# Attention with a gated expert layer: laying out the keys and queries of the first two pairs by products with the identity

## The chip, the cores and the metric

The kernel runs on one core of one Trainium2 chip. The metric is the device time of one execution in microseconds (us); three executions of the kernel before took 623.07, 626.6 and 625.8 us, with a median of 625.8.

## What is computed

Inputs are q, k and v of 4 batches, 8 heads, 576 positions and 64 dimensions, in float32. The reference, cut to what matters:

```
scores = q @ k.T / 8
x      = log1p(|i - j|) / log1p(max(i, 1))           # one number per pair of positions
bias   = relu(x * w1 + b1) @ w2                       # 32 hidden units, 8 heads
attn   = softmax(scores + bias);  y = attn @ v        # y: 2304 tokens x 512
e      = argmax(y @ w_gate)                           # one of 8 experts per token
out    = gate * sigmoid((y @ w_output_gate)[e]) * (relu(y @ w1[e]) @ w2[e])
```

## The kernel before

The program has three parts in order of time. The first, up to about 75 us, makes the bias of all heads, once for all batches. The second walks through 16 pairs of heads (4 batches x 4 pairs) and makes attention. The third runs the experts on groups of 288 tokens. Each engine issues its instructions in the order in which the code emits them, and so does SyncE (SP), which only issues transfers. A wait is set automatically wherever data or a buffer needs one.

**Bias rows.** A loop over 36 steps `r16` (line 957) makes 16 rows of positions in each step. `emit_hid` (713) makes four tiles of hidden units, two steps ahead; the digits of `ON_ACT` (71) say how many of the four ScalarE makes, VectorE makes the rest. The tile `hid` has three buffers. `emit_bias` (730) has TensorE multiply them by `w2` into one of two PSUM banks (tag `s`, shared with the scores), ScalarE evicts the result into one of four places (`evs`, line 731: step r uses the place of step r-4), and SyncE stores it from there into `bias`.

**Work laid between the bias rows.** `BEGIN` (66) names what is begun after which step: `l` and `L` load the second and third pair (`emit_load`, 758, two SyncE transfers of k and q into one tile `nat`, of which there is one buffer, line 159); `k0` to `k2` and `K0` to `K2` lay out the first and the second pair in three chunks; `p0` to `p2` and `P0` to `P2` move parts of them; `s0` to `s3` make the first scores, `z` copies a part of the queries on GpSimd, `v` loads the values. What a step begins is finished in the next step, after that step's `emit_hid` and ahead of its `emit_bias`. Behind the loop the string `FIRST` (52) orders the rest of the first pair; its `k0++`, `k1++`, `k2++` lay out the third pair, which must have been loaded by then.

**Keys and queries.** The score product wants three operands of 128 partitions: the keys rounded, twice, one copy in each half of 64 partitions; the keys' remainder, twice; and the queries, rounded above and their remainder below. `emit_kq` (798) transposes one chunk of `nat` (keys above, queries below), ScalarE writes the rounded values (`hi`), VectorE the remainder (`lo`). `emit_place` (812) then moves halves to where they belong with SyncE transfers of 288 KB, four for a pair: two in `p0`, one in `p1` that overwrites what `p0` reads, one in `p2`.

Of the kernel before, what the change touches and what calls it, by code (L numbers as in the profile page):

```python
# [9 lines left out]
F32 = mybir.dt.float32  # L10
F32R = mybir.dt.float32r
# [3 lines left out]
ACTF = mybir.ActivationFunctionType  # L15
ALU = mybir.AluOpType
# [4 lines left out]
B, H, S, D = 4, 8, 576, 64  # L21
# [42 lines left out]


BEGIN = {
    3: "k0", 4: "k1", 5: "k2 l", 7: "p0", 9: "p1", 13: "p2 K0", 14: "z", 16: "K1", 17: "s0", 20: "K2",
    21: "L", 22: "s2 s1", 29: "P0", 32: "s3 P1", 35: "v P2",
}

ON_ACT = "210210000111121212102110310010201111"
# [63 lines left out]
def attention_moe_kernel(  # L135
# [15 lines left out]
    nc = tc.nc  # L151
    V = nc.vector
# [19 lines left out]
    def cn(name):  # L172
        o, n = _WHERE[name]
        return kept[:, o:o + n]

    ident = cn("ident")
# [8 lines left out]
    def psum_t():  # L185
        return ps_t.tile([128, 512], F32, name="pt", tag="t")
# [485 lines left out]
    with ExitStack() as actx:  # L672
        pool = lambda name, bufs, **kw: actx.enter_context(tc.tile_pool(name=name, bufs=bufs, **kw))
        kq = pool("kq", 2)
# [81 lines left out]
        kl_t, v_t, vb_t, nat_t = {}, {}, {}, {}  # L756

        def emit_load(b, pr):
            t = nat_t[b, pr] = nat.tile([128, 9, 2, D], F32, name="nat", tag="nat")
            for i, x in enumerate((k, q)):  # L760
                nc.sync.dma_start(
                    out=t[:, :, i, :],
                    in_=x[b, 2 * pr:2 * pr + 2].rearrange("h s d -> (h s) d").rearrange("(n p) d -> p n d", p=128),
                )

        def emit_load_v(b, pr):
            vt = vp.tile([128, 9, D], F32, name="vt", tag="v")
            nc.sync.dma_start(
                out=vt, in_=v[b, 2 * pr:2 * pr + 2].rearrange("h s d -> (h s) d").rearrange("(n p) d -> p n d", p=128)
            )  # L770
            v_t[b, pr] = vt
# [26 lines left out]
        def emit_kq(b, pr, c):  # L798

            hi, lo = (t[(b * NPAIR + pr) % 2][:, c * 384:c * 384 + 384] for t in (kh2, qs2))  # L800
            pt = psum_t()
            for i in range(3):
                nc.tensor.transpose(  # L803
                    pt[:, i * 128:i * 128 + 128], nat_t[b, pr][:, c * 3 + i].rearrange("p t d -> p (t d)"), ident
                )
            nc.scalar.activation(out=hi, in_=pt[:, 0:384], func=ACTF.Copy, scale=cn("ksc"))
            yield
            V.scalar_tensor_tensor(
                out=lo, in0=pt[:, 0:384], scalar=cn("ksc"), in1=hi.bitcast(F32), op0=ALU.mult, op1=ALU.subtract
            )  # L810

        def emit_place(b, pr, i):

            hi, lo = (t[(b * NPAIR + pr) % 2] for t in (kh2, qs2))
            if i == 0:
                kl_t[b, pr] = kq.tile([128, 2 * S], F32R, name="kl", tag="kt")
            kl, up, down = kl_t[b, pr], slice(0, 64), slice(64, 128)
            for to, src in (((kl[up], lo[up]), (kl[down], lo[up])), ((lo[up], hi[down]),), ((hi[down], hi[up]),))[i]:
                nc.sync.dma_start(out=to.bitcast(F32), in_=src.bitcast(F32))

        def emit_q4(b, pr):
            nc.gpsimd.tensor_copy(
                out=q4.rearrange("p (a c) -> p a c", c=64)[:, 0::3, :],
                in_=qs2[(b * NPAIR + pr) % 2].rearrange("p (h c) -> p h c", h=2)[:, :, 512:S].bitcast(F32),
            )
# [14 lines left out]
        def emit_s(b, pr, qb, hl):  # L840
            h = 2 * pr + hl
            if b not in sums_t:
                sums_t[b] = st_p.tile([128, 4, H], F32, name="sums", tag="sums", bufs=2)
                sums4_t[b] = st_p.tile([128, NPAIR], F32, name="sums4", tag="sums4", bufs=2)
            e_t[b, pr, qb] = e_all[qb]
            ps = ps_s.tile([128, 2, 512], F32, name="ps", tag="s")
            kt, qs = (x[(b * NPAIR + pr) % 2] for x in (kh2, qs2))
            low = kl_t[b, pr]
            o = hl * S + qb * 128
            k0 = hl * S  # L850
            for c in range(2):
                for n, keys in enumerate((kt, low)):
                    nc.tensor.matmul(  # L853
                        ps[:, c, 0:288], lhsT=qs[:, o:o + 128], rhs=keys[:, k0 + c * 288:k0 + c * 288 + 288],
                        start=n == 0, stop=n == 1,
                    )
            yield
            softmax_rows(e_t[b, pr, qb][:, hl, :], ps, bias[qb][:, h, :], sums_t[b][:, qb, h:h + 1])
# [66 lines left out]
        pairs = [(b, pr) for b in range(B) for pr in range(NPAIR)]  # L925
        begun = " ".join(BEGIN.values()).split()

        def begin(op):
            if op[0] == "k":
                return emit_kq(*pairs[0], int(op[1]))  # L930
            elif op[0] == "p":
                emit_place(*pairs[0], int(op[1]))
            elif op[0] == "s":
                return emit_s(*pairs[0], int(op[1]) // 2, int(op[1]) % 2)
            elif op[0] == "K":
                return emit_kq(*pairs[1], int(op[1]))
            elif op[0] == "P":
                emit_place(*pairs[1], int(op[1]))
            elif op in "lL":
                emit_load(*pairs[1 + (op == "L")])  # L940
            elif op == "v":
                emit_load_v(*pairs[0])
            elif op == "z":
                emit_q4(*pairs[0])
            return iter(())
# [11 lines left out]
        for r16 in range(36):  # L957
            if r16 < 34:
                hids.append(emit_hid(r16 + 2))

            for g in halfway:
                finish(g)
            halfway.clear()
            emit_bias(r16, hids.pop(0))
            for op in BEGIN.get(r16, "").split():
                g = begin(op)
                next(g, None)
                halfway.append(g)
# [3 lines left out]
        for hl in range(2):  # L972
            for i, w in enumerate((wg, wog)):
                nc.sync.dma_start(
                    out=wgb[hl * 64:hl * 64 + 64, :, hl * 16 + i * 8:hl * 16 + i * 8 + 8],
                    in_=w.rearrange("(a t d) e -> t d a e", t=2, d=64)[hl],
# [24 lines left out]
        for n in range(len(pairs) + 1):  # L1001
            todo = {i: 1 for i in range(8)}
            for op in orders.get(n, ORDER).split():
                name = op.rstrip("+-")
# [19 lines left out]
                b, pr = pairs[m]  # L1024
                i = int((name + "0")[1])
# [12 lines left out]
                elif name[0] == "t":  # L1038
                    emit_t(
                        b, pr, i, int(name[2]), copies("a" if name[0:3] in to_act and b == B - 1 and m < len(pairs) - 1 else name[3])  # L1040
                    )
                elif name[0] == "a":
                    emit_av(b, pr, i, copies(name[2]))
                    if i == 2 and m == len(pairs) - 2:
                        emit_zb(*pairs[-1])
                    if pr == NPAIR - 1:
                        work.append(emit_logits(b, i))
                        if i == 2:
                            work.append(emit_route(b))
                            if b >= B - 2:  # L1050
                                work.append(route_group(b - (B - 2)))
                elif name[0] in "kp":
                    if name[0] == "p":
                        emit_place(b, pr, i)
                    else:
                        finish(emit_kq(b, pr, i))
                else:
                    {"l": emit_load, "v": emit_load_v, "c": emit_z, "b": emit_load_vb, "g": emit_zb, "z": emit_q4}[name](b, pr)
# [201 lines left out]
```

## Time and profile before

| | before |
|---|---|
| median of three executions | 625.8 us |
| profiled execution | 619.93 us, of which the span 617.8 |
| TensorE products (PE) | 576.8 us busy, 93% of the span |
| weight loads (PEld) | 489.2 us, 79% |
| VectorE (DVE) | 413.1 us, 67% |
| ScalarE (ACT) | 375.2 us, 61% |
| GpSimd (POOL) | 94.7 us, 15% |
| chain that ended last | PE 76%, no visible wait 6%, DVE 6%, DMA 5%, ACT 4% |

The profile describes one execution; its span runs from the first instruction to the last. Busy shares are means over parts of the program with different limits. Products overlap in the array, so TensorE's busy time also covers the latency of single products. A float32 product of the bias rows stands in the trace as two records.

### The profile page before, as it was taken

To read this page: it belongs to the slowest core of one execution; us is meant where nothing else is said; L and a number is where in the kernel's file an instruction comes from. 1 tells how busy PE (TensorE), PEld (TensorE's weight loads), DVE (VectorE), ACT (ScalarE), POOL (GpSimd) and SP (SyncE) were. 2 spreads that over 40 slices of the span, in tenths; PEclk is the share of its full clock that TensorE was granted. 3 is DMA by queue.
4 is the path that set the end of the run, shared out by engine and by line. 5 is a ranking of instruction groups with operands and counts; after the bars stand their busy time and mean duration, and the time that the engine had idled before them with its cause. 6 is when DMAs were issued, how large, how long until landed. Compare 5 with 4: busy or idle time off the path is not lost.

```text
span 617.8 us, 13534 instructions
## 1 busy us (share of the span) xinstructions
PE 576.8 (93%) x5070; PEld 489.2 (79%) x5070; DVE 413.1 (67%) x974; ACT 375.2 (61%) x774; POOL 94.7 (15%) x172
## 2 busy tenths in 40 slices
PE   4868799999999999999999899999999999999992
PEld 2323478888888778887777668999999999999992
DVE  6967676666777677776678756767777665555521
ACT  5788677777776677777677554535445454545410
POOL 1000000000010000100002382040404132120202
PEclk9988899999999999999999999999999999999997
DMA  6998976564566754586435675566666574756521
GB/s 142 228 204 191 228 161 140 125 135 102 125 140 167 157 123 109 116 211 134 108 102 130 199 256 179 173 213 197 199 185 203 174 221 145 248 158 181 168 69 48
DMA packets 99093, 100.26 MB, mean 162 GB/s; under 512 B 71319, under 2 KB 71575, under 8 KB 99016
## 3 DMA queue, kind: packets, MB, share of 16 engines
q1 hardware_dynamic: 93028, 84.93, 54.6%
q0 software_dynamic: 3232, 9.64, 4.9%
q10 hardware_dynamic: 2756, 4.72, 2.2%
q8 instruction: 42, 0.69, 0.5%
q14 instruction: 35, 0.29, 0.2%
HBM read 60.34 MB, written 9.50 MB: 113 GB/s over the span
## 4 chain that ended last, share of the span: by engine, by line
PE 76%; issue 6%; DVE 6%; DMA 5%; ACT 4%; POOL 1%; POOLq 0%; SPq 0%; DVEq 0%; ACTq 0%
PE p L1114 15%; PE p L1137 15%; PE pa L922 13%; PE ps L853 9%; PE pt L890 9%; PE pb L735 2%; PE ps L869 2%; PE pt L803 2%; DVE e L833 2%; DMA bias<-evh 2%; DVE hid L724 2%; PE pt L655 1%; PE pt L1156 1%; PE pt L902 1%; PE pt L515 1%
## 5 line engine op out<-in xcount | busy, mean ns | idle before, releaser
L838 ACT ACTIVATE e<-e,nm 128x576 f32<-128x576 f32 x144 | 111.3, 773 | 48.9 <-DVE nm L833 47.5
L833 DVE CUSTOM_DVE_ANT_0 e<-ps,bias 128x576 f32<-128x576 f32 x144 | 105.5, 751 | 32.4 <-PE ps L853 28.5
L1114 PE MATMUL p<-x,w 128*128 128x288 f32 x768 | 105.7, 296 | 0.0
L1114 PEld LDWEIGHTS p<-x,w 128*128 128x128 f32 x768 | 102.8, 188 | 0.5 <-issue 0.4
L890 PE MATMUL pt<-kept,e 128*128 128x128 f32 x576 | 82.8, 277 | 2.8 <-ACT et L894 1.2
L853 PE MATMUL ps<-qt,qs 128*128 128x288 f32 x256 | 79.3, 329 | 4.4 <-DVE nm L833 3.0
L890 PEld LDWEIGHTS pt<-kept,e 128*128 128x128 f32 x576 | 65.3, 141 | 18.0 <-issue 8.1
L1137 PE MATMUL p<-hh,w2h 128*128 128x288 f32 x256 | 77.3, 302 | 0.0
L1137 PE MATMUL p<-hl,w2h 128*128 128x288 f32 x256 | 75.6, 295 | 0.0
L1137 PE MATMUL p<-hh,w2l 128*128 128x288 f32 x256 | 75.3, 294 | 0.0
L922 PE MATMUL pa<-et,vt 128*64 128x256 f32 (+1 forms) x640 | 73.2, 354 | 0.1
L853 PE MATMUL ps<-kl,qs 128*128 128x288 f32 x256 | 70.8, 294 | 0.0
L894 ACT COPY et<-pt 128x512 f32<-128x512 f32 (+1 forms) x105 | 57.4, 566 | 14.5 <-PE pt L890 14.4
L735 PE MATMUL pb<-hid,w2blk 128*32 128x288 f32 x576 | 49.5, 459 | 16.8 <-DVE hid L724 7.6
L922 PEld LDWEIGHTS pa<-et,vt 128*64 128x64 f32 x640 | 42.6, 136 | 22.0 <-issue 5.7
L853 PEld LDWEIGHTS ps<-qt,qs 128*128 128x128 f32 x256 | 48.2, 188 | 8.4 <-DVE nm L833 4.5
L735 PEld LDWEIGHTS pb<-hid,w2blk 128*32 128x32 f32 x576 | 20.2, 120 | 42.3 <-DVE hid L724 10.9
L1080 POOL DMA_INDIRECT out_dram<-y,sidx x22 | 26.3, 1195 | 178.1 <-DVE y L1159 149.9
L1116 ACT ACTIVATE hh<-p 128x288 fp32r<-128x288 f32 x64 | 26.2, 411 | 44.7 <-PE p L1114 42.0
L724 DVE TENSOR_SCALAR hid<-e,early 128x576 f32<-128x576 f32 x110 | 48.3, 510 | 6.7 <-PE pb L735 3.5
L1137 PEld LDWEIGHTS p<-hh,w2h 128*128 128x128 f32 x256 | 48.0, 188 | 0.6 <-issue 0.6
L487 DVE TENSOR_TENSOR w2l<-w2r,w2h 128x1024 fp32r<-128x1024 f32 x32 | 39.2, 1225 | 13.9 <-ACT w2h L486 13.8
(218 smaller groups left out, 969.7 us busy)
## 6 DMA issues: line engine op xcount, KB each, us to landing
w1r<-in_moe_w_dram SPq DMA_DIRECT2D x36, 512.0 KB, 3.8
w2r<-in_moe_w_dram SPq DMA_DIRECT2D x36, 512.0 KB, 4.0
kl<-qs SPq DMA_DIRECT2D x32, 288.0 KB, 5.2
nat<-in_k_dram SPq DMA_DIRECT2D x16, 288.0 KB, 3.8
nat<-in_q_dram SPq DMA_DIRECT2D x16, 288.0 KB, 5.2
bias<-evh SPq DMA_DIRECT2D x16, 288.0 KB, 4.5
bias<-evl SPq DMA_DIRECT2D x16, 288.0 KB, 5.0
qs<-qt SPq DMA_DIRECT2D x16, 288.0 KB, 3.2
```

Source lines behind the costliest of these rows:

```text
L487: V.tensor_tensor(out=lo, in0=src, in1=hi.bitcast(F32), op=ALU.subtract)
L724: V.tensor_scalar(out=to, in0=src, scalar1=bc[:, r:r + 1], scalar2=0.0, op0=ALU.add, op1=ALU.max,)
L735: nc.tensor.matmul(pb[32 * t:32 * t + 32, c, 0:288], lhsT=w2f, rhs=hids[t][:, c * 288:c * 288 + 288], start=True, stop=True,)
L833: V.tensor_tensor_reduce(out=e.rearrange("p (a j) -> p a j", a=2), in0=ps[:, :, 0:n], in1=bias_ap.rearrange("p (a j) -> p a j", a=2), scal ...
L838: nc.scalar.activation(out=e, in_=e, func=ACTF.Exp, scale=-1.0, bias=nm, accum_out=sum_ap)
L853: nc.tensor.matmul(ps[:, c, 0:288], lhsT=qs[:, o:o + 128], rhs=keys[:, k0 + c * 288:k0 + c * 288 + 288], start=n == 0, stop=n == 1,)
L890: nc.tensor.transpose(pt[:, n * 256 + j * 128:n * 256 + j * 128 + 128], es[j][:, (n0 + n) * 128:(n0 + n) * 128 + 128], ident,)
L894: copy(out=et[:, n0:n0 + nn, :].rearrange("p n s -> p (n s)"), in_=pt[:, 0:nn * 256])
L922: nc.tensor.matmul(pa[p:p + 64, 0:n], lhsT=values, rhs=weights, start=i == 0, stop=i == 4)
L1080: p = nc.gpsimd.indirect_dma_start(out=out, out_offset=bass.IndirectOffsetOnAxis(ap=idx, axis=0), in_=y[0:n], in_offset=None, bounds_check ...
L1114: nc.tensor.matmul(p1[:, 0:CH], lhsT=w[:, fs], rhs=x[:, c, :], start=n == 0, stop=n == 11)
L1137: nc.tensor.matmul(p2[:, 0:CH], lhsT=w[f // 2][:, f % 2, ds], rhs=x[f], start=n == 0, stop=n == 23)
```

## The change

For the first two pairs, `emit_kq` hands over to a new function. It makes no transposes: for keys and then for queries it multiplies the chunk by the identity with ordinary float32 products of 64 columns of weights, once into partitions 0 to 63 and once into 64 to 127. ScalarE writes the rounded keys and the rounded queries to both halves, VectorE the keys' remainder to both halves (`kl`) and the queries' remainder over the lower half. Nothing of these pairs is moved by transfers any more. `BEGIN` is written anew: `l` after step 5 ahead of `k0`, `k1`, `k2` after steps 7, 9 and 11; `K0`, `K1`, `K2` after 19, 25 and 28; the third pair's load `L` after the last step, ahead of `v`. All other pairs are laid out as before.

```
 BEGIN = {
-    3: "k0", 4: "k1", 5: "k2 l", 7: "p0", 9: "p1", 13: "p2 K0", 14: "z", 16: "K1", 17: "s0", 20: "K2",
-    21: "L", 22: "s2 s1", 29: "P0", 32: "s3 P1", 35: "v P2",
+    5: "l", 7: "k0", 9: "k1", 11: "k2", 13: "z", 17: "s0", 19: "K0", 22: "s2 s1", 25: "K1", 28: "K2",
+    32: "s3", 35: "L v",
 }
...
         def emit_kq(b, pr, c):
             hi, lo = (t[(b * NPAIR + pr) % 2][:, c * 384:c * 384 + 384] for t in (kh2, qs2))
+            if (b, pr) in pairs[0:2]:
+                yield from emit_kq_twice(b, pr, c, hi, lo)
+                return
...
+        def emit_kq_twice(b, pr, c, hi, qs):
+            if c == 0:
+                kl_t[b, pr] = kq.tile([128, 2 * S], F32R, name="kl", tag="kt")
+            kl = kl_t[b, pr][:, c * 384:c * 384 + 384]
+            pts = []
+            for x, to, scale in ((0, hi, 1.0), (1, qs, 0.125)):
+                pt = psum_t()
+                for i in range(3):
+                    for half in (0, 64):
+                        nc.tensor.matmul(
+                            pt[half:half + 64, i * 128:i * 128 + 128], lhsT=nat_t[b, pr][:, c * 3 + i, x, :],
+                            rhs=ident, start=True, stop=True,
+                        )
+                nc.scalar.activation(out=to, in_=pt[:, 0:384], func=ACTF.Copy, scale=scale)
+                pts.append(pt)
+            yield
+            V.tensor_tensor(out=kl, in0=pts[0][:, 0:384], in1=hi.bitcast(F32), op=ALU.subtract)
+            down = slice(64, 128)
+            V.scalar_tensor_tensor(
+                out=qs[down], in0=pts[1][down, 0:384], scalar=0.125, in1=qs[down].bitcast(F32),
+                op0=ALU.mult, op1=ALU.subtract,
+            )
...
         def begin(op):
-            elif op[0] == "p":
-                emit_place(*pairs[0], int(op[1]))
...
-            elif op[0] == "P":
-                emit_place(*pairs[1], int(op[1]))
```

## Rows read from the trace of the kernel before

**Rows 1.** Busy time by stretch: PE, PEld, DVE, ACT, POOL, TensorE clock, DMA share, GB/s.

```profile
14.50:26.00 11.50, 11.20 (x133) 5.17 (x133) 11.50 (x27) 9.29 (x15) 0.00 (x0) 1.00 0.98 223
26.00:42.00 16.00, 10.37 (x115) 3.63 (x106) 10.79 (x25) 12.47 (x20) 0.29 (x1) 0.89 0.94 209
...
55.50:69.80 14.30, 12.05 (x148) 5.63 (x140) 14.27 (x34) 11.73 (x17) 0.00 (x0) 0.98 0.81 200
...
76.00:375.00 299.00, 289.70 (x2596) 235.80 (x2594) 212.22 (x567) 210.18 (x490) 43.87 (x117) 1.00 0.61 146
```

**Rows 2.** SyncE's queue: start us, us, line, transfer, count.

```profile
19.29 0.53 SPq L761 DMA_DIRECT2D nat<-in_k_dram  x1
...
20.86 2.38 SPq L745 DMA_DIRECT2D bias<-evl  x2
23.33 1.43 SPq L819 DMA_DIRECT2D kl<-qs  x2
...
31.89 0.49 SPq L819 DMA_DIRECT2D qs<-qt  x1
...
74.85 2.44 SPq L748 DMA_DIRECT2D bias<-evl  x4
77.34 0.59 SPq L768 DMA_DIRECT2D vt<-in_v_dram  x1
```

**Rows 3.** What SyncE waited for, 0 to 90 us: total us, times, longest us.

```profile
SPq L819 <- DMA kl<-qs: 4.3, 2, 4.1
SPq L761 <- PE pt L803: 2.1, 1, 2.1
```

**Rows 4.** ScalarE in order of time; in brackets the idle time before, and its releaser.

```profile
32.58 0.74 ACT L739 ACTIVATE evh<-pb,early 128x576 f32<-128x576 f32 x1 [2.25 <-DMA bias<-evh]
33.22 1.43 ACT L722 ACTIVATE hid<-e,early 128x576 f32<-128x576 f32 x2
34.55 0.73 ACT L739 ACTIVATE evh<-pb,early 128x576 f32<-128x576 f32 x1
35.17 0.58 ACT L806 ACTIVATE qt<-pt,kept 128x384 fp32r<-128x384 f32 x1
35.64 0.78 ACT L722 ACTIVATE hid<-e,early 128x576 f32<-128x576 f32 x1
...
41.16 0.74 ACT L739 ACTIVATE evh<-pb,early 128x576 f32<-128x576 f32 x1
```

**Rows 5.** VectorE in order of time.

```profile
9.50 7.38 DVE L724 TENSOR_SCALAR hid<-e,early 128x576 f32<-128x576 f32 x17
...
35.78 0.62 DVE L808 SCALAR_TENSOR_TENSOR qs<-pt,kept,qt 128x384 fp32r<-128x384 f32 x1 [3.39 <-ACT qt L806]
36.32 2.32 DVE L724 TENSOR_SCALAR hid<-e,early 128x576 f32<-128x576 f32 x5
```

**Rows 6.** TensorE's products in order of time.

```profile
13.40 1.18 PE L735 MATMUL pb<-hid,w2blk 128*32 128x288 f32 x16 [0.22 <-ACT evh L739]
...
42.40 0.37 PE L853 MATMUL ps<-qt,qs 128*128 128x288 f32 x1 [1.38 <-DMA qt<-qt]
...
81.93 0.49 PE L803 MATMUL pt<-kept,nat 128*128 128x128 f32 x3
```

**Rows 7.** Weight loads of value products with 64 columns, alternating halves.

```profile
99.60 0.14 PEld L922 LDWEIGHTS pa<-et,vt 128*64 128x64 f32 x1
99.61 0.14 PEld L922 LDWEIGHTS pa<-et,vb 128*64 128x64 f32 x1
99.66 0.14 PEld L922 LDWEIGHTS pa<-et,vt 128*64 128x64 f32 x1
```

**Rows 8.** Transfers issued near 52.7, 24.8 and 19.9 us: count, size, us to landing.

```profile
bias<-evl SPq DMA_DIRECT2D x2, 288.0 KB, 3.1
...
bias<-evh SPq DMA_DIRECT2D x1, 288.0 KB, 7.6
...
nat<-in_q_dram SPq DMA_DIRECT2D x1, 288.0 KB, 5.8
```

**Rows 9.** What ScalarE waited for, 7 to 76 us: total us, times, longest us.

```profile
ACT evh L739 <- DMA bias<-evh: 2.6, 2, 2.2
```

## The prediction

> **What bounds the kernel now.** I read the page first: TensorE is busy for 93% of the span, and from 76 us on it is busy almost without a break [rows 1]. Whatever delays the start of that steady part therefore moves the end by as much; whatever is done beside it costs next to nothing. The change touches only the stretch ahead of it, where the 36 bias rows are made. There no engine is full throughout: at 26 to 42 us VectorE works 10.8 of 16 us and ScalarE 12.5, while at 55.5 to 69.8 us VectorE works 14.27 of 14.30 us [rows 1]. So the stretch has two limits in turn: first waits, then VectorE.
>
> To see the first one I read SyncE's queue. Every store of a bias row goes through it, in the order of the code, and one that must wait holds all behind it. The move `p1` sits in that queue until the two moves `p0` have landed: it is issued only at 31.89 us [rows 2], the queue stood 4.1 us for it at once and 4.3 in all [rows 3], and ScalarE's eviction at 32.58 us had waited 2.25 us for an older store [rows 4]. Bias row r is evicted into the place of row r-4 (line 731, four places), so an eviction can run only once the store of four rows before has landed. That chain is what the change alters in both directions. Last, TensorE's first score product at 42.40 us waited 1.38 us for the move `p2` [rows 6].
>
> **What goes.** Eight SyncE moves of 288 KB (four for each of two pairs), with the 2.25 us stall and the 1.38 us wait. ScalarE's waits for stores on evh over the stretch sum to 2.6 us, most of it that one stall [rows 9], so the other moves hold nobody visibly and I credit them with nothing (0.4 us at most).
>
> **What is added per chunk.** Three transposes become 12 products, each recorded twice as other float32 products here are: 24 records. The trace has no such product from this line; the nearest are the value products with 64 columns of weights that go to the two partition halves in turn: loads of a pair start 0.01 us apart and pairs follow each other every 0.05 to 0.06 us at 64 moving columns [rows 7], 28 ns a record. At 128 columns I take double, 56 ns, so 1.3 us a chunk. If every load stood by itself (0.14 us each), it would be 3.3 us; below the transposes' own time it can't be. ScalarE gets a second copy, 0.47 us from start to start (35.17 to 35.64) [rows 4]. VectorE gets a second subtraction of 384 elements a partition, 0.54 us from start to start [rows 5]; 64 partitions instead of 128 I price the same. Bounds for each: nothing, where the engine waits anyway, and the full 0.47 or 0.62.
>
> The Trainium skill ("TensorE: Matmul & The Clock Gate", section "The mechanism") says that weight loads overlap running products only where their row groups differ; all loads here use all the rows. By that rule loads and products alternate. The rows speak against it; its price is the fourth rival.
>
> **The step that decides: `l` now stands ahead of `k0` to `k2`.** The first pair's tile and the second pair's share one buffer (pool `nat`, one buffer, line 159). Before, the second load stood behind the last reader in the code. Now it is emitted at row 5, and the readers k0, k1, k2 come at rows 7, 9 and 11. It may not overwrite what they read, so it must wait for k2's last product, and SyncE keeps its order: the stores of rows 6 to 11 are queued behind it. That a load of `nat` does wait for the readers of the pair ahead, on this queue, is in the trace (2.1 us on line 803) [rows 3]. When does k2 end? VectorE makes its hid parts at 0.434 us (17 in 7.38) and has those of row 6 done at 16.88 [rows 5]. Rows 7 to 11 need 4+4+3+3+3 = 17 more on VectorE (line 71): 7.4 us, plus k0's two subtractions, 1.1: 25.3 us. Row 11's products take 1.2 us [rows 6], k2 follows with 1.3: about 28.0 us. Then SyncE issues the two loads, 1.57 us (19.29 to 20.86) [rows 2], and row 6's store at 29.6. Landing: 3.1 us in a quiet queue, 7.6 behind two moves, and 5.8 for a load of the same size behind another [rows 8]; I take 5.5, near the last. Row 10's eviction, which needs row 6's place, starts at about 35.1 us. ScalarE is through with what it may do ahead of it by about 26 us: some 9 us of nothing. Neither VectorE (hid has three buffers) nor TensorE (two banks) can run far ahead.
>
> From there ScalarE is the limit: evictions of rows 10 to 17, 8 x 0.63 = 5.0 us (34.55 to 35.17) [rows 4]; the hid parts of rows 13 to 18 that it makes, 9 x 0.67 = 6.0 (33.22 to 34.55 for two) [rows 4]; k2's two copies, 0.9. Row 17 is out at 35.1 + 12.0 = 47.1 us, against 41.16 + 0.63 = 41.8 [rows 4]. Row 17's products need the bank of row 15, free 1.9 us before that, at 45.2; s0 follows one row of products later, at 46.2, against 42.40 [rows 6], since no move is waited for now. **First term: +3.8 us** (with a landing of 3.1 us +1.4, of 7.6 us +5.9, and a us either way for k2).
>
> **Second pair's chunks, later.** K0 goes from row 13 to 19, K1 from 16 to 25, K2 from 20 to 28. At row 19 ScalarE is busy without a break, and K0's two copies stand against K2's one: **+0.5 us** (0 to 1). K1 and K2 fall into the stretch where VectorE is full and had no chunk before: 4 x 0.54 = **+2.2 us** (0 if the waits around s1 to s3 take them in, 2.4 at 0.61 each). Scores s0 to s3 keep their rows and so their waits.
>
> **Third pair's load.** `L` goes from row 21 to behind row 35, ahead of `v`. SyncE is done with the last rows' stores at 74.85 + 2.44 = 77.3 us [rows 2]; the two loads then take 1.5 us to issue and 5 to 6 to land, the later one at about 83.5. Its first reader is at 81.93 [rows 6], in TensorE's order, with the transposes of the first pair behind it. Some idle there is shared with waits on ScalarE: **+1.2 us** (0 to 2.5). `v`, issued 1.5 us later than its 77.34 [rows 2], lands about 85, before its own products.
>
> **The sum.** 3.8 + 0.5 + 2.2 + 1.2 = +7.7 us (terms together from about 0.5 to 13). The profiled execution took 619.93 us (617.8 of span and 2.1 around it), so by it 627.6. That execution is 5.9 us below the median of the three runs; on the median: 625.8 + 7.7 = 633.5 us.
>
> **Rivals.**
> 1. *Transfers are the bound, and fewer of them pay for all.* The 16 queues are busy for 0.98 and 0.94 of the time from 14.5 to 42 us [rows 1], and the moves are 2.4 MB at about 210 GB/s, so 11 us of transfer time go. Were every row limited by that, the 8 to 9 us stall would be more than made up: about 3 us faster, 622.8. It decides from where the lost transfer time exceeds the stall. For it: the share near 1. Against it: ScalarE hardly waits for stores [rows 9], and the new stall leaves these same queues empty for some 4 us. Chance 0.13.
> 2. *The stall is taken in.* Before also lost time between 26 and 56 us, and waits around the scores may shrink when the work behind them comes late; with a landing of 3.1 us and K1, K2 in gaps the sum is 1.4 + 0.5 = 1.9, so 627.7. For it: VectorE idles 5 of 16 us at 26 to 42 [rows 1]. Against it: ScalarE's chain after the stall has no gaps. Chance 0.20.
> 3. *It costs more.* The stores of rows 6 to 9 arrive bunched, 7.6 us like the worst row, the late load costs its 2.5 us, and TensorE comes out of 7 us of idle at the lower clock (0.89 granted in 26 to 42 now [rows 1]): 5.9 + 1 + 2.4 + 2.5 + 1 = 12.8, so 638.6. Chance 0.12.
> 4. *Loads don't overlap.* Each chunk then takes 3.3 us; k1 and k2 stand ahead of the waiting load, 2 us each, so +4: 637.5. Against it stand the pairs 0.01 us apart [rows 7]. Chance 0.05.
>
> That the load does not hold SyncE at all would be the change not doing what I read in it; then only rival 1 is left, and its chance holds this.
>
> **Chances and range.** The forecast has 0.50; its own range is 628 to 639. About 0.5% (3.1 us) is what a measurement of this kernel can tell from no change. Faster by more than that: most of rival 1, 0.11. Within it: the rest of rival 1, rival 2 and the forecast's low edge, 0.24. Slower: 0.65. The range for 8 in 10 reaches down through rival 2 to the edge of rival 1, and up through rivals 3 and 4: 622.5 to 641.
>
> **What would show it.** In the changed kernel's trace: SyncE's two loads of the second pair issued near 28 us, with no store between about 18 and 29 us; one idle time of ScalarE of 7 to 10 us ahead of an eviction, ended by a store; first score product near 46 us, with no wait for a move; VectorE full from about row 23 to 32; TensorE's first transposes of the third pair waiting for `nat`; steady part starting near 82 us. Wrong if the loads are issued near 18 us or the stores of rows 6 to 9 go out as before: then the first term is gone and the time is near 626 or below.

## The result, and the profile after

The changed kernel took 632.12 us (median of four executions, 631.2 to 634.02), the kernel before 625.13 us (four, 623.07 to 626.6): a ratio of 1.012 with an interval of [1.0085, 1.0155]. Measured a second time it was 1.0103 [1.0078, 1.0128]. It is slower, by 6.4 to 7.5 us as these ratios give it; the forecast was +7.7 us.

The profiled execution took 631.2 us, its span 629.2, at a granted clock of 0.987 in the mean (0.985 before). First part of the page of the changed kernel: busy time, share of the span, instructions.

```profile
PE 581.3 (92%) x5196; PEld 494.4 (79%) x5196; DVE 417.4 (66%) x980; ACT 377.4 (60%) x780; POOL 95.0 (15%) x172
```

Against before, busy time grew by 4.5 us for TensorE's products, 5.2 for its weight loads and less for the others, much of it the added work itself, so the page alone does not tell where 7 us went. Changed kernel, busy time by stretch, columns as in [rows 1]:

```profile
14.50:26.00 11.50, 11.42 (x168) 6.69 (x172) 11.44 (x27) 8.56 (x16) 0.00 (x0) 1.00 0.48 129
26.00:42.00 16.00, 7.87 (x96) 3.32 (x90) 7.94 (x18) 7.81 (x13) 0.29 (x1) 0.79 0.73 166
...
82.00:381.00 299.00, 288.72 (x2587) 235.00 (x2583) 212.21 (x566) 211.11 (x491) 42.81 (x115) 1.00 0.61 147
```

At 26 to 42 us TensorE, VectorE and ScalarE all do less than before, ScalarE 7.81 us against 12.47, and the 16 DMA engines are at 0.73 against 0.94 [rows 1]. The three engines wait there at once. The steady part, 299 us of it, is what it was (288.7 us of products, 289.7 before). SyncE's queue shows for what they wait; from the first 90 us of the changed kernel, columns as in [rows 2]:

```profile
16.66 1.50 SPq L745 DMA_DIRECT2D bias<-evh  x2
28.29 0.38 SPq L761 DMA_DIRECT2D nat<-in_k_dram  x1
28.72 0.60 SPq L761 DMA_DIRECT2D nat<-in_q_dram  x1
29.41 1.64 SPq L745 DMA_DIRECT2D bias<-evl  x2
31.14 1.34 SPq L745 DMA_DIRECT2D bias<-evh  x2
...
82.15 2.46 SPq L748 DMA_DIRECT2D bias<-evl  x4
84.70 0.54 SPq L761 DMA_DIRECT2D nat<-in_k_dram  x1
```

From 18.2 to 28.3 us SyncE issues nothing: the load of the second pair, first in its order, waits for the last product that reads the shared tile. The stores of rows 6 to 9 stand behind it and go out in a bunch. ScalarE in the changed kernel, in order of time, with the idle time before an instruction in brackets:

```profile
25.80 0.82 ACT L722 ACTIVATE hid<-e,early 128x576 f32<-128x576 f32 x1
34.81 0.74 ACT L739 ACTIVATE evl<-pb,early 128x576 f32<-128x576 f32 x1 [8.19 <-DMA bias<-evl]
35.45 1.43 ACT L722 ACTIVATE hid<-e,early 128x576 f32<-128x576 f32 x2
...
45.30 0.76 ACT L739 ACTIVATE evh<-pb,early 128x576 f32<-128x576 f32 x1
```

One eviction waits 8.19 us for a store that was issued late; from there to 45.3 us ScalarE has no gap. TensorE's products in the changed kernel:

```profile
26.72 1.53 PE L825 MATMUL pt<-kept,nat 128*64 128x128 f32 x24
35.60 5.19 PE L735 MATMUL pb<-hid,w2blk 128*32 128x288 f32 x48 [7.35 <-ACT evl L739]
...
46.12 0.40 PE L880 MATMUL ps<-qt,qs 128*128 128x288 f32 x1
...
82.18 0.40 PE L880 MATMUL ps<-qt,qs 128*128 128x288 f32 x1
...
89.89 0.52 PE L806 MATMUL pt<-kept,nat 128*128 128x128 f32 x3 [0.49 <-DMA nat<-in_q_dram]
```

The 24 records end at 28.25 us, and the load goes out at 28.29. The second row is the next three bias rows, for which TensorE had idled 7.35 us. The third is the first score product, which no longer waits for a move (42.40 us in [rows 6]), the fourth the first product of the steady part, the last one the third pair's first transposes. For the steady part, the answering product of the kernel before, with the three bias rows ahead of it:

```profile
70.51 4.42 PE L735 MATMUL pb<-hid,w2blk 128*32 128x288 f32 x48 [2.53 <-DVE nm L833]
74.88 0.40 PE L853 MATMUL ps<-qt,qs 128*128 128x288 f32 x1
```

VectorE in the changed kernel, the stretch behind the scores s2 and s1:

```profile
60.12 4.82 DVE L724 TENSOR_SCALAR hid<-e,early 128x576 f32<-128x576 f32 x11 [1.28 <-PE pb L735]
64.85 0.55 DVE L832 TENSOR_TENSOR kl<-pt,qt 128x384 fp32r<-128x384 f32 x1
65.44 0.56 DVE L834 SCALAR_TENSOR_TENSOR qs<-pt,qs 64x384 fp32r<-64x384 f32 x1
66.03 4.38 DVE L724 TENSOR_SCALAR hid<-e,early 128x576 f32<-128x576 f32 x10
70.44 0.56 DVE L832 TENSOR_TENSOR kl<-pt,qt 128x384 fp32r<-128x384 f32 x1
71.03 0.56 DVE L834 SCALAR_TENSOR_TENSOR qs<-pt,qs 64x384 fp32r<-64x384 f32 x1
71.63 5.25 DVE L724 TENSOR_SCALAR hid<-e,early 128x576 f32<-128x576 f32 x12
76.91 0.76 DVE L860 CUSTOM_DVE_ANT_0 e<-ps,bias 128x576 f32<-128x576 f32 x1
```

The same stretch in the kernel before:

```profile
55.53 14.26 DVE L724 TENSOR_SCALAR hid<-e,early 128x576 f32<-128x576 f32 x33 [2.25 <-PE pb L735]
69.70 0.74 DVE L833 CUSTOM_DVE_ANT_0 e<-ps,bias 128x576 f32<-128x576 f32 x1
```

In the changed kernel VectorE runs without a gap from 60.12 us on, with the four added subtractions inside, 0.59 us each from start to start (those that work on 64 partitions save nothing). From the start of the run to the reduction of the next scores it takes 16.79 us, 14.17 before.

The delay against the kernel before grows in steps that can be read off: first score +3.72 us (42.40 to 46.12), VectorE's run behind the scores +4.59 (from 55.53 in the trace before to 60.12), steady part +7.30 (74.88 to 82.18), third pair's transposes +7.96 (81.93 to 89.89). The spans differ by more, 11.4 us. Of that, 8.3 us are there at the first expert product (372.81 and 381.12 us); the last 3.1 come in the expert part, whose code no edit touches and which took 244.9 to 248.7 us in the profiled executions of this study (245.0 in that of the kernel before). So the 7.0 us between the medians is the better figure for the change.

### The profile page after: what moved, and what is told of

Its sections match the earlier page's. It is cut to its first block, busy times and chain, and to the rows that moved or that the text cites. A ratio compares the mean times of both kernels' runs of the same rounds, so it can differ in the third digit from the quotient of the medians.

```text
span 629.2 us, 13782 instructions
## 1 busy us (share of the span) xinstructions
PE 581.3 (92%) x5196; PEld 494.4 (79%) x5196; DVE 417.4 (66%) x980; ACT 377.4 (60%) x780; POOL 95.0 (15%) x172
## 5 line engine op out<-in xcount | busy, mean ns | idle before, releaser
L735 PE MATMUL pb<-hid,w2blk 128*32 128x288 f32 x576 | 47.0, 454 | 21.9 <-ACT evl L739 8.1
L880 PEld LDWEIGHTS ps<-kl,qs 128*128 128x128 f32 x256 | 48.4, 189 | 0.0
```

Source lines behind the costliest of these rows:

```text
L735: nc.tensor.matmul(pb[32 * t:32 * t + 32, c, 0:288], lhsT=w2f, rhs=hids[t][:, c * 288:c * 288 + 288], start=True, stop=True,)
L880: nc.tensor.matmul(ps[:, c, 0:288], lhsT=qs[:, o:o + 128], rhs=keys[:, k0 + c * 288:k0 + c * 288 + 288], start=n == 0, stop=n == 1,)
```

## Experiments

The experiments ran in three groups, each on one chip together with the kernel before: 1 to 4, 5 to 8, 9 and 10. Ratios are to the kernel before of the same group, with 95% intervals. Its median was 625.13 us in the first group, 624.32 in the second and 620.94 in the third, so kernels of different groups are compared by ratio. Times inside a kernel are from one profiled execution each; how far those can differ for the same code is said where it matters. Line numbers move by a few from kernel to kernel.

**1. The load behind its readers.**

```
-    5: "l", 7: "k0", 9: "k1", 11: "k2", 13: "z", ...
+    7: "k0", 9: "k1", 11: "k2 l", 13: "z", ...
```

> The changed kernel with one word moved: the second pair's load is emitted behind its buffer's last reader (after step 11, behind k2) instead of ahead of the readers (after step 5). Theory A (the load holds SyncE's queue, and with it the stores of the bias rows, until k2): the two loads are still issued near 27 to 28 us, but the stores of rows 6 to 9 go out between 18 and 26 us, ScalarE's idle time of 8.2 us ahead of row 10's eviction is gone (under 1.5 us left), the first scores come near 40 us instead of 46.1, the part of the 16 pairs starts near 76 us instead of 82.2; time 6 us less than the changed kernel, 625 to 627 us, level with the kernel before. Rival B (the slowdown is the extra work of the products, copies and subtractions, and the wait only shows where it falls): the idle time moves elsewhere and the time stays at 631 to 633 us.

Measured: 624.39 us, ratio 0.9981 [0.9956, 1.0006]. One word moved takes the whole loss away, 1.2 to 1.4% by the ratios; 625 to 627 us had been expected. SyncE's queue in this kernel:

```profile
18.89 2.25 SPq L744 DMA_DIRECT2D bias<-evl  x2
23.23 1.83 SPq L744 DMA_DIRECT2D bias<-evh  x2
26.77 2.49 SPq L744 DMA_DIRECT2D bias<-evl  x2
29.35 0.54 SPq L760 DMA_DIRECT2D nat<-in_k_dram  x1
```

The load is issued 1.1 us later than in the changed kernel, but the stores of rows 6 to 11 now go out ahead of it. TensorE in this kernel: first score, the three bias rows ahead of the steady part, and its first product.

```profile
37.87 0.40 PE L879 MATMUL ps<-qt,qs 128*128 128x288 f32 x1 [0.67 <-ACT evh L738]
...
69.99 3.27 PE L734 MATMUL pb<-hid,w2blk 128*32 128x288 f32 x48 [2.77 <-DVE nm L859]
73.19 0.40 PE L879 MATMUL ps<-qt,qs 128*128 128x288 f32 x1
```

The first score is 8.25 us earlier than in the changed kernel and 4.53 us earlier than in the kernel before. So the +3.72 us is the sum of two larger things: the held queue costs 8.25, and the rest of the change gains 4.53. Experiments 2 and 7 have the same code up to there and their first scores at 38.91 and 38.62 us, so a single trace gives these figures only to about 1 us: 7.2 to 8.25 of cost, 3.5 to 4.5 of gain. From the first score to the three bias rows ahead of the steady part it takes 32.1 us, 31.6 in the changed kernel, 28.1 before (42.40 to 70.51): the added work and the second pair's chunks, which all stand there now, cost 3.5 to 4.0 us and use up most or all of the gain. That these rows then take 3.27 us and not 4.42 is another matter (last section).

**2. Both loads early, behind their readers.** Besides, the third pair's load goes from step 35 to 28, behind the second pair's last chunk.

```
-    7: "k0", 9: "k1", 11: "k2 l", ... 28: "K2", 32: "s3", 35: "L v",
+    7: "k0", 9: "k1", 11: "k2 l", ... 28: "K2 L", 32: "s3", 35: "v",
```

> As the run before it, and the third pair's load is emitted behind K2 (after step 28) instead of behind the last bias row. Theory A with my term for the late load: the wait of 0.49 us of the third pair's first transposes for nat is gone, and the time is 0.5 us (0 to 1.2) below that of the run with the second pair's load moved alone, so about 625 us. Rival: the load now runs among the bias rows' stores and delays an eviction, 0 to 1 us slower.

Measured: 623.84 us, 0.9978 [0.9956, 0.9999], the lowest ratio of the study, with an upper end that all but touches 1. The third pair's transposes follow the steady part's first product after 7.06 us here (75.00 to 82.06), after 7.77 in experiment 1 (73.19 to 80.96) and 7.05 before: the late load costs 0.7 us in the trace. Between the times of experiments 1 and 2 (0.03%) that can't be seen.

**3. Products at the old steps.**

```
-    7: "k0", 9: "k1", 11: "k2 l", 13: "z", 17: "s0", 19: "K0", 22: "s2 s1", 25: "K1", 28: "K2 L", ...
+    3: "k0", 4: "k1", 5: "k2 l", 13: "K0", 14: "z", 16: "K1", 17: "s0", 20: "K2", 21: "L", 22: "s2 s1", ...
```

> The products in place of the moves, and nothing else: k0, k1, k2 and the second pair's load at their old steps 3, 4, 5; K0, K1, K2 at 13, 16, 20; the third pair's load at 21. Theory A: the method itself is no loss; the 2.25 us stall for a store behind the moves and the 1.38 us wait of the first score are gone, the extra copies (6 x 0.37 us) and subtractions (6 x 0.57 us) lie mostly beside waits; K1 and K2 are out of the stretch where VectorE is full; time 2 us (0 to 5) below the kernel before, 620 to 625 us, and 7 to 12 us below the changed kernel. Rival B (the added work is what costs): 3 us or more above the kernel before, 628 us or more.

Measured: 626.06 us, 1.0023 [0.9996, 1.0049]. A miss: 620 to 625 us had been expected, and it is 0.45% above experiment 2 with no held queue. ScalarE in this kernel, from the evictions of rows 4 to 6:

```profile
17.34 0.74 ACT L738 ACTIVATE evh<-pb,early 128x576 f32<-128x576 f32 x1 [0.71 <-PE pb L734]
...
22.60 0.74 ACT L738 ACTIVATE evl<-pb,early 128x576 f32<-128x576 f32 x1 [0.71 <-PE pb L734]
```

They wait for TensorE, which must do a chunk of 24 records and a bias row in each of these steps; in the kernel before the same three evictions had idled 0.42, 0.37 and 0.74 us, the last for a store. The first score is 1.8 us later than in experiment 2 (38.91):

```profile
40.73 0.40 PE L879 MATMUL ps<-qt,qs 128*128 128x288 f32 x1
```

Against the kernel before it is only 1.67 us earlier, though nothing is moved here and no score waits for a move. So the 3.5 to 4.5 us of experiment 1 are not the gain of doing without moves alone: about half of it or more comes with the later chunks, of which K0 and K1 leave the stretch ahead of the first score. Besides, the three bias rows ahead of the steady part take 5.99 us where experiment 1 has 3.27 (the last section has the clock in both); this profile is of the slowest of its twelve executions, 628.98 us. Which half of the edit costs what was left to experiments 9 and 10.

**4. The readers earlier, the load still ahead.**

```
-    5: "l", 7: "k0", 9: "k1", 11: "k2", ...
+    5: "l", 7: "k0", 8: "k1", 9: "k2", ...
```

> The changed kernel with the load still emitted after step 5, ahead of its readers, but the readers k1 and k2 two steps earlier (after 8 and 9 instead of 9 and 11). Theory A: the loads are issued when k2 is done, some 2.5 to 3 us earlier (25.5 us instead of 28.3), ScalarE's idle time ahead of an eviction falls from 8.2 to about 5.5 us, and the time by 2 to 3 us, to 629 to 630. Rival B: no change, 631 to 633.

Measured: 629.98 us, 1.0079 [1.0054, 1.0105], in between, as it must be if the wait counts from the last reader, and in the range expected (629 to 630). SyncE and ScalarE in this kernel:

```profile
27.28 0.38 SPq L760 DMA_DIRECT2D nat<-in_k_dram  x1
```

```profile
33.65 0.74 ACT L738 ACTIVATE evl<-pb,early 128x576 f32<-128x576 f32 x1 [5.21 <-DMA bias<-evl]
```

The load leaves 1.0 us earlier than in the changed kernel, where 2.5 to 3 had been expected; the eviction starts 1.16 us earlier, the first score 1.46 (44.66 us). The idle time fell by 3.0 us, as expected, but for another reason in part: ScalarE's last work ahead of it ends 1.8 us later, since the last chunk's two copies are now in it and wait for TensorE.

**5. The load early, into a place of its own.** The second pair's tile is laid into a buffer that nothing uses yet; `BEGIN` stays as in the changed kernel.

```
-            t = nat_t[b, pr] = nat.tile([128, 9, 2, D], F32, name="nat", tag="nat")
+            if (b, pr) == pairs[1]:
+                t = e_all[2].rearrange("p h s -> p (h s)").rearrange("p (n t d) -> p n t d", n=9, t=2)
+            else:
+                t = nat.tile([128, 9, 2, D], F32, name="nat", tag="nat")
+            nat_t[b, pr] = t
```

> The changed kernel with every instruction in its old place, the second pair's load after step 5 included; only the bytes that this load writes are others (the tile of exponentials of the third query block, not used until the bias rows are done), so that it has no reader to wait for. Theory A (it is the wait for the shared buffer, and SyncE's order, that cost the time): the loads are issued near 17 to 18 us, ScalarE's idle time of 8.2 us is gone, the first scores come near 38 to 39 us, time 624 to 626 us, as with the load emitted behind k2. Rival B (a load at this place is bad in itself, by the transfers that it puts among the first stores, or the products are): 629 us or more.

Measured: 624.03 us, 0.9996 [0.9974, 1.0018]. SyncE and ScalarE in this kernel:

```profile
18.55 1.10 SPq L765 DMA_DIRECT2D e<-in_k_dram  x1
19.70 0.87 SPq L765 DMA_DIRECT2D e<-in_q_dram  x1
21.28 2.90 SPq L745 DMA_DIRECT2D bias<-evl  x2
```

```profile
20.51 0.75 ACT L739 ACTIVATE evl<-pb,early 128x576 f32<-128x576 f32 x1 [2.56 <-DMA bias<-evl]
```

The same load at the same place in the order, without a buffer to wait for, goes out at 18.55 us and the stores behind it at once. The first score is at 38.74 us, the loss is gone. It is the wait for the shared buffer, then, and not the place of the load in the code. Its transfers still make row 6's eviction wait 2.56 us.

**6. The kernel before, with its load moved ahead of its three readers.**

```
-    3: "k0", 4: "k1", 5: "k2 l", ...
+    2: "l", 3: "k0", 4: "k1", 5: "k2", ...
```

> The kernel before, with its transposes and moves, and one word moved: the second pair's load after step 2, ahead of the readers of its buffer (k0 to k2 after steps 3 to 5), instead of behind k2. Theory A: the loads are issued where they were, near 19.3 us, but the stores of rows 3 to 5 are now queued behind them, issued at 21 to 22.5 us instead of 16 to 19; row 7's eviction, which needs row 3's place, starts near 25.5 us instead of 21.15; 3 to 5 us slower than the kernel before, less what its later stall for the moves takes in: 627 to 630 us. Rival B (such an order does no harm without the products): 624 to 626 us.

Measured: 627.0 us, 1.0043 [1.0019, 1.0067]: slower by 2.7 us in the medians (3 to 5 had been expected), with none of the other edits. ScalarE in this kernel:

```profile
25.00 0.74 ACT L739 ACTIVATE evl<-pb,early 128x576 f32<-128x576 f32 x1 [4.00 <-DMA bias<-evl]
```

Row 7's eviction waits 4.00 us for a store that stands behind the load, so the order alone brings the mechanism. The wait is shorter here, where the last reader comes three steps behind the load and not six.

**7. More hidden units on ScalarE in VectorE's full stretch.** On top of experiment 2, one tile more of each of the rows 26, 27, 29 and 31.

```
-ON_ACT = "210210000111121212102110310010201111"
+ON_ACT = "210210000111121212102110311111211111"
```

> The version with both loads behind their buffer's readers, and four hid parts of rows 26, 27, 29 and 31 made by ScalarE instead of VectorE. If VectorE is what the stretch from row 23 to 32 waits for, as the term for K1 and K2 had it (4 x 0.59 us of subtractions fall there), 4 x 0.434 = 1.7 us leave it and the time falls by 0.5 to 1.7 us, to 622 to 623.5 us. Rival: ScalarE's evictions come later by the 0.67 us of each part and nothing is won: 623.5 to 625 us.

Measured: 623.36 us, 0.9981 [0.9962, 0.9999]; by the ratio no gain over experiment 2. In the trace the third pair's transposes come 1.3 us earlier (80.73 us against 82.06), 0.3 of it already at the first score, where the code is still the same; so little of it, if any, reaches the end.

**8. The changed kernel again,** unaltered, beside experiments 5 to 7.

> The changed kernel itself, unaltered, to compare the others with on the same chip: 631 to 633 us, 1.0 to 1.3% above the kernel before. All theories expect the same; a ratio under 1.006 would say that the first measurement overstated the loss.

Measured: 631.92 us, 1.0103 [1.0078, 1.0128]. The wait is there again, 8.01 us, and the first score at 46.14; the first expert product comes at 383.14 us against 381.12, so single executions of one kernel differ by 2 us in that mark.

**9 and 10. The two halves of experiment 3.** Experiment 9 has its second pair's steps (13, 16, 20, load 21) with the first pair's of experiment 2, experiment 10 the other way round.

```
+    7: "k0", 9: "k1", 11: "k2 l", 13: "K0", 14: "z", 16: "K1", 17: "s0", 20: "K2", 21: "L", ...
...
+    3: "k0", 4: "k1", 5: "k2 l", 13: "z", 17: "s0", 19: "K0", 22: "s2 s1", 25: "K1", 28: "K2 L", ...
```

> First pair's chunks after steps 7, 9, 11 with the load behind them, as in e2_both_loads_early; second pair's chunks after 13, 16, 20 and the third pair's load after 21, as in e3_products_at_old_steps. What made e3 2.2 us slower than e2 (626.06 against 623.84)? Theory A, the first pair's products in steps 3 to 5, where ScalarE's evictions came to wait 0.71 us each for TensorE: then this kernel has none of it, 623.2 to 624.4 us, and the evictions of rows 4 to 6 show no such waits. Theory B, the second pair's early chunks: they take ScalarE's and VectorE's time ahead of the scores, and the first row behind the scores waits longer for nm: 625.6 to 626.6 us, with the steady part near 78 us. Between 624.6 and 625.4: both have a share.

> The other half of e3_products_at_old_steps alone: first pair's chunks after steps 3, 4, 5 with the load of the second behind them; second pair's after 19, 25, 28 with the third pair's load behind the last, as in e2_both_loads_early. Theory A (first pair's products in steps 3 to 5 cost): 625.6 to 626.6 us, with the 0.71 us waits of the evictions of rows 4 to 6 for TensorE. Theory B (second pair's early chunks cost): 623.2 to 624.4 us, though these waits stand here too. Between: a share each.

Measured: experiment 9 624.76 us, 1.0063 [1.0038, 1.0089]; experiment 10 621.62 us, 1.001 [0.9984, 1.0035]. The bounds expected were in microseconds of the first group, where the kernel before took 4.2 us more; by ratio they would be 629.1 and 625.8 us there. Experiment 10 then stands where theory A puts it, but its interval overlaps those of experiments 2 and 3. Its trace has the waits of 0.71 us for TensorE in steps 3 to 5, and the first score 0.7 us later than in experiment 2 (39.60 and 38.91), less than the 1.0 us by which the first scores of experiments 1 and 2 differ with the same code. Its steady part starts 1.9 us later, but 1.5 of that is one group of three bias rows (from 52.37 us) that takes 4.81 us at a low granted clock and 3.29 in experiment 2; experiment 1, which has none of the early products, shows the 4.81 there too, so this part is not theirs. Experiment 9 does not test theory B as it was meant to, since it has a wait that experiment 3 does not have and that I had not thought of. TensorE in experiment 9:

```profile
27.34 1.53 PE L824 MATMUL pt<-kept,nat 128*64 128x128 f32 x24
28.80 2.15 PE L734 MATMUL pb<-hid,w2blk 128*32 128x288 f32 x32
34.48 1.55 PE L824 MATMUL pt<-kept,nat 128*64 128x128 f32 x12 [3.54 <-DMA nat<-in_k_dram]
```

With the load behind step 11 and its reader at step 13, the products wait 3.54 us for the data, with the bias rows in order behind them. The changed kernel's early load and this one are the two ends of one choice: ahead of the readers it holds the stores, close ahead of its own use it is late. So which half of experiment 3's edit costs its 0.45% stays open: by the ratios, experiment 10 stands 0.32% above experiment 2 and 0.13% below experiment 3, with intervals of 0.2 to 0.3% either way.

## Why the prediction was right, step by step

| step | predicted | changed kernel | again (experiment 8) |
|---|---|---|---|
| last reader done, load issued (us) | 28.0, 28.0 | 28.25, 28.29 | 28.40, 28.44 |
| row 6's store issued | 29.6 | 29.41 | 29.56 |
| from that issue to row 10's eviction | 5.5 | 5.40 | 5.27 |
| row 10's eviction | 35.1 | 34.81 | 34.83 |
| ScalarE idle ahead of it | about 9 | 8.19 | 8.01 |
| first score | 46.2 (+3.8) | 46.12 (+3.72) | 46.14 (+3.74) |
| one chunk's 24 records | 1.3 | 1.46 | 1.46 |
| second pair's chunk at row 19 | +0.5 | +0.87 | +1.68 |
| four subtractions in VectorE's full stretch | +2.2 | +2.62 | +2.83 |
| third pair's late load | +1.2 | +0.66 | +0.55 |
| sum at the third pair's transposes | +7.7 | +7.96 | +9.17 |

The terms are differences to the one profile of the kernel before. The row-19 term is what the start of VectorE's run is later by, less the first term; the sum also holds what the three bias rows ahead of the steady part took longer, 0.1 and 0.4 us.

**The deciding step held.** The load waits for its buffer at the head of an in-order queue, the stores behind it are late, and ScalarE's evictions wait for their places. Experiments 1, 4, 5 and 6 show it from four sides: it goes with the order, shrinks when the last reader comes earlier, goes with another buffer, and comes into the kernel before with the order alone. Each time in the chain came out within 0.3 us but for the idle time, and experiment 8 repeats it: ScalarE's durations and the row rate had been read from the stretch itself.

**A size that the net hid.** The prediction credited the moves that go with nothing beyond the stall and the wait (0.4 us at most). Its first term was worked out as a time on the clock (46.2 us), not as cost less gain, and so took in whatever else changes ahead of the first score. Experiment 1 puts the two apart: 7.2 to 8.25 us of cost, 3.5 to 4.5 of gain. The stall of 2.25 and the wait of 1.38 [rows 4, 6] are 3.63 us, but they are not the gain as such: both are gone in experiment 3 too, with the chunks at their old steps, and its first score is only 1.67 us ahead of before. The prediction has no term for what K0 and K1 free when they leave that stretch.

**VectorE's full stretch** cost 2.62 us as the four instructions at 0.59 do (2.36) and a little more; nothing took them in. The chunk at row 19 was undersized by 0.4 us in one execution and 1.2 in the other. Ahead of that stretch VectorE waits 2.07 us for TensorE in the second and 2.25 in the kernel before, but 1.28 in the first, so this term is not known to better than 0.8 us. The late load was oversized by about 0.6: its second half was issued at 85.29 us and the transposes that read it started at 89.89, 4.6 us later, where 5 to 6 had been taken for the landing.

**How much of it was luck.** The chain up to the first score was not: it came out twice, step by step. That the whole sum came within 0.3 us of the first trace was in part, since its later terms were off by 0.4 to 0.6 us in both directions, and experiment 8 has 9.17 at the same mark.

**Slips in the working.** None moves the sum by as much as those. The parts of the time for k2 (25.3, 1.2 and 1.3 us) make 27.8, not 28.0. "First waits, then VectorE" leaves out that VectorE was full from 14.5 to 26 us as well (11.50 of 11.50 us [rows 1]); the time for k2 does go by VectorE's rate. [rows 9] has the waits for the `evh` places alone; those for `evl` add 1.1 us in two, 0.74 ahead of all moves and 0.31 behind them. And the landing of 3.1 us [rows 8] belongs to a store issued at about 56.3 us and not near 52.7; it is the later time that bears out the quiet queue.

**The rivals.** That transfers are the bound is refuted by the changed kernel: the 16 DMA engines were busy at 0.48 and 0.73 from 14.5 to 42 us where they had been at 0.98 and 0.94 [rows 1], with the program slower; and when the held queue is taken away in experiment 1 they are at 0.80 and 0.88 with the first score 4.5 us ahead of before. That the stall would be taken in fell with the first score. That it would cost more fell with the landing (5.40 us, not 7.6) and the late load (0.66, not 2.5); TensorE did come out of its idle time at a low clock, but at no cost (last section). That loads don't overlap is refuted by the rows of experiment 9: 24 records start to next in 1.46 us (27.34 to 28.80), not 3.3. Weight loads in the changed kernel:

```profile
26.72 1.29 PEld L825 LDWEIGHTS pt<-kept,nat 128*64 128x64 f32 x24 [0.47 <-issue]
```

All 24 loads lie in 1.29 us beside the products. The Trainium skill's rule ("TensorE: Matmul & The Clock Gate", section "The mechanism"), that loads overlap only where row groups differ, is not what this trace shows for loads that use all rows and go to the two column halves in turn. The same section also lets a load go ahead of running products where it goes to the background weight buffer, and by that they may overlap; no run here shows into which buffer they went.

**What was not shown:** why the forecast's base was right. The sum was added to the median of the kernel before and not to its profiled execution, which at 619.93 us lies below all four timed ones; on that base the forecast would have been 627.6 us. That execution's expert part took 245.0 us. So did those of experiments 9 and 10 (245.0 and 244.9), in the group where the kernel before had its median at 620.94 us, while all other profiles had 247.1 to 248.7. The profile of before may come from a chip like that group's, but no run tested it.

## What to carry to other kernels

A load that is moved forward in the code doesn't start earlier if its buffer is still being read, and on a queue that keeps its order everything behind it waits as well; look for the last reader of the buffer, and put the load just behind it or give it a buffer of its own. Work out such a chain in times on the clock, from durations of the same stretch, and then split it into cost and gain by an experiment: here one word in the schedule decided between 1.2% slower and no loss. A saving made ahead of a stretch in which another engine is full can be paid back by what is added to that engine there, as the four subtractions did here. And one trace gives a mark only to about 1 us, so a small difference between two kernels needs more than one trace of each.

## What the runs showed of the hardware

- The same three bias rows ahead of the steady part, which follow a wait of 2.1 to 2.8 us for the softmax in all twelve profiles, take very different times in single executions: 3.27 us in three of them, 4.42 to 5.99 in the other nine. Busy time over just these rows, columns as in [rows 1], in experiment 1, in the kernel before, in experiment 10 and in experiment 3:

```profile
70.00:73.20 3.20, 3.20 (x49) 1.36 (x49) 0.00 (x0) 2.32 (x4) 0.00 (x0) 1.00 0.02 5
```

```profile
70.50:74.90 4.40, 4.39 (x49) 1.82 (x49) 0.00 (x0) 2.34 (x4) 0.00 (x0) 0.69 1.03 233
```

```profile
72.20:77.00 4.80, 4.80 (x49) 2.13 (x49) 0.00 (x0) 2.32 (x4) 0.00 (x0) 0.64 0.57 148
```

```profile
73.00:79.00 6.00, 5.97 (x49) 2.22 (x49) 0.00 (x0) 2.35 (x4) 0.00 (x0) 0.50 0.20 54
```

TensorE is full in each, and the time goes with the granted clock, from its upper level throughout (1.00, 2.4 GHz) to the lower one throughout (0.50, 1.2 GHz): 3.2, 4.4, 4.8 and 6.0 us for the same work. The transfers don't explain it: their share is 0.02 in the first, 1.03 in the second and 0.20 in the last. The length of the wait doesn't decide it: it was 2.77 us in experiment 1, with 3.27 us for the rows, and in experiment 2, with 4.66; what does stays open. So 1 to 2.8 us of the difference between two single profiles can be this alone. Steps have to be read ahead of these rows, and even there the first scores of experiments 1, 2 and 7 differ by 1.0 us with the same code.
- A low clock need not cost anything. The three rows right behind the long idle time of the changed kernel:

```profile
35.60:40.80 5.20, 5.19 (x48) 1.60 (x48) 2.82 (x6) 5.20 (x10) 0.29 (x1) 0.61 0.72 172
```

They are at 0.61, between the two levels, but ScalarE works 5.20 of 5.20 us there and sets the pace; this is why the forecast's first term held without a price for the clock.
- A subtraction over 64 partitions took VectorE as long as one over 128, 384 elements each: 0.56 and 0.55 us.
